# A table that moves 1119 operations in the instruction lists of a scheduled attention and two-MLP kernel

## The chip, the cores and the metric

The kernel runs on one core of one Trainium2 chip. The metric is the device time of one execution in microseconds (us). Five instruction lists run side by side, each strictly in its own order: TensorE (PE, matmuls), VectorE (DVE), ScalarE (ACT), GpSimd (POOL) and SyncE (SP, which issues every DMA here). An instruction at the head of a list that still waits for data holds up all that stand behind it.

## The reference

Three stages follow each other; all arrays are float32.

```python
# attention, 8 x 8 heads, 576 rows in chunks of 64, head size 64
scores = scale * np.matmul(q_c, k_c.transpose(0, 1, 2, 4, 3))
scores = scores - np.max(scores, axis=-1, keepdims=True)
attn = np.exp(scores)
attn = attn / (np.sum(attn, axis=-1, keepdims=True) + 1e-09)
out = np.matmul(attn, v_c)
# first MLP on 4608 tokens of 512: 512 -> 1536 (twice) -> 512
g = x @ w_gate
silu = g * (1.0 / (1.0 + np.exp(-g)))
x = silu * (x @ w_val) @ w_out
# second MLP: 512 -> 2048 -> 512
h = x @ w_in
g = h * (1.0 / (1.0 + np.exp(-1.702 * h)))
return g @ w_out
```

## The kernel before, in words

Tokens are worked in nine blocks of 512. There are four passes over all blocks: passes 0 and 1 hold six 128-wide slices each of `w_gate` and `w_val` and are the first MLP, passes 2 and 3 hold eight slices of `w_in` and are the second. Pass 0 also carries the attention: while PE multiplies block b, the 36 attention units of 128 tokens that feed the later blocks pass through it in small pieces (scores L662, values L667, transposes L732, the softmax on DVE at L715 to L723 with its exponential on ACT at L718). The first product of pass 0 starts at 23.0 us; the second MLP starts at 947.3 us and its second pass at 1303.9 us.

A float32 operand is split into a rounded high half and a remainder ("hi" and "lo"), and three matmuls take the place of one (`mm3`, L406 to L408). The high half is a copy on ACT (L390); the low half is a subtraction (`tt`, L399), on DVE or on POOL as the call says. Weights come from DRAM as 64-bit words and are made float32 on the core by two ACT and two DVE instructions (`conv_part`, L476 to L484). From the second block on, each 2x2 block product is done with seven multiplications in place of eight, so sums and differences of the weight quarters (`combos_from_quarters`) and of the token quarters (`token_combos`) have to be made first. The weights that later passes need are made during pass 0 and pass 2 and stored to DRAM (`group_to_dram`).

The order of all 6704 operations is set by a planner in the kernel, `Program`. Each operation is recorded with an engine, an estimated duration, a priority, and the operations it depends on. `order` lists the operations by priority and readiness under those estimates; `dues` works out latest times backwards, and the priorities are drawn towards them. This is repeated 28 times, each result is played through once more in `replay`, and the best of the 28 is emitted. The engine of an operation is fixed by the call that records it.

Of the kernel before, what the change touches and what calls it, by code (L numbers as in the profile page):

```python
# [24 lines left out]
def rd(ap):  # L25
    return ap.bitcast(F32)

# [68 lines left out]
class Program:  # L96
# [9 lines left out]
    ROUNDS = 14  # L106
    BEAT = 3.413
# [111 lines left out]
    def replay(self, seq, seed):  # L219
        jitter = random.Random(seed)  # L220
        queue = {eng: [] for eng in self.FREE}
        for o in reversed(seq):
            queue[o.eng].append(o)
            o.end = None
        free, table, port, owner, moved = dict(self.FREE), None, 0.0, None, 0.0
        busy, clock, beat = {}, 0.5, 0
        left, last = len(seq), 0.0
        while left:
            pick = None
            for eng, todo in queue.items():  # L230
                if not todo or any(d.end is None for d in todo[-1].deps):
                    continue
                o = todo[-1]
                s = max([free[eng], *(d.end + self.hop(d, o) for d in o.deps)])
                if pick is None or s < pick[0]:
                    pick = s, o
            s, o = pick
            queue[o.eng].pop()
            left -= 1
            us = o.us  # L240
            if o.eng == "dma":
                free["dma"] = s + 0.47
                moved = max(s + 1.5, moved) + 0.95 * us
                o.end = moved + 1.4 + max(-1.2, jitter.gauss(0, 0.8))
                continue
            if o.eng == "pe":
                while beat < s // self.BEAT:
                    share = busy.get(beat, 0.0) / self.BEAT
                    clock = 1.0 if share > 0.85 else 0.5 if share < 0.5 else clock
                    beat += 1  # L250
                if clock < 1.0 and us < 3.0:
                    us *= 1.8
                t = s
                while t < s + us:
                    k = t // self.BEAT
                    e = min(s + us, (k + 1) * self.BEAT)
                    busy[k] = busy.get(k, 0.0) + e - t
                    t = e + 1e-9
            if o.table and o.table != table:
                s, table = s + self.LOAD, o.table  # L260
            if o.port:
                us += abs(jitter.gauss(0, 0.02))
                o.end = max(s + 0.1, port + (self.HAND if o.eng != owner and port > s + 0.05 else 0.0)) + us - 0.1
                port, owner = o.end - 0.1, o.eng
            else:
                o.end = s + us
            free[o.eng] = o.end - (0.05 if o.eng != "pe" else 0.0)
            last = max(last, o.end)
        return last

    def emit(self):
        for o in self.ops:
            o.key, o.after = o.prio, []
        for o in self.ops:
            for d in (*o.deps, *o.follows):
                d.after.append(o)
        best = None
        for i in range(2 * self.ROUNDS):
            if i == self.ROUNDS:
                for o in self.ops:  # L280
                    o.key = o.prio
            seq = self.order()
            self.dues(seq)
            last = sum(self.replay(seq, j) for j in range(3)) / 3
            if best is None or last < best[0]:
                best = last, seq
            for o in self.ops:
                if o.prio < 9999:
                    o.key += (o.due - o.key) / (2 if i < self.ROUNDS else 4)
        for o in best[1]:  # L290
            o.fn()
# [3 lines left out]
def attention_two_moe_kernel(ctx: ExitStack, tc: tile.TileContext, q, k, v, wg, wv, wo, wi, wo2, out):  # L295
# [100 lines left out]
    def tt(dst, a, b, by, n, prio, eng="dve", of_a=lambda ap: ap, of_b=lambda ap: ap, near=None):  # L396
        e = nc.vector if eng == "dve" else nc.gpsimd
        op(eng, dve_us(n) if eng == "dve" else pool_us(n),
           lambda: e.tensor_tensor(out=dst.ap, in0=of_a(a.ap), in1=of_b(b.ap), op=by), [a, b], [dst], prio, near=near)  # L399
# [43 lines left out]
    for p, (layer, gs) in enumerate(passes):  # L443
        start.append([])
        for b in range(NB):
            start[p].append(t)
            t += sum(step_us(g) for g in gs) + (8.0 if p == 0 and b < NB - 1 else 0) + (3 * GV if p == b == 0 else 0)
# [244 lines left out]
    def scores(un, prio, done=None):  # L692
# [3 lines left out]
        if done is None:  # L696
            op("pe", 0.8, lambda: score_blocks(un), [un.q, un.k], [un.s], prio)
        else:
            done.o = right(t)

            def both_blocks():
                value_blocks(done)
                score_blocks(un)

            op("pe", 1.3, both_blocks, [done.v, done.e, un.q, un.k], [done.o, un.s], prio, near=1.0)
            attended(done, prio)
# [49 lines left out]
    def alone(un, prio):  # L756
        un.o = right(two(un))
        op("pe", 0.8, lambda: value_blocks(un), [un.v, un.e], [un.o], prio, near=1.0)
# [585 lines left out]
```

## Time and profile before

| what | value |
|---|---|
| median of 3 runs | 1688.71 us (1688.47 to 1689.58) |
| profiled execution | 1689.54 us, span 1687.2 us |
| PE busy | 1658.1 us (98% of the span) |
| PE weight loads busy | 1579.5 us (94%) |
| DVE busy | 1098.8 us (65%), 1606 instructions |
| ACT busy | 892.2 us (53%), 1511 instructions |
| POOL busy | 726.0 us (43%), 736 instructions |
| mean granted PE clock | 0.996 of full speed |

The profiled execution lies 0.83 us above the median; 2.3 us of it lie outside the span. PE is the bound nearly everywhere, so what matters is where it is not busy, or busy without being at its peak. Because matmuls overlap, a stalled PE can still be shown as busy; the weight-load column (PEld) is a second measure of it. PE's work is the same in both kernels.

### The profile page before, as it was taken

How to read it: one execution, taken by the hardware profiler on the slowest of the kernel's cores; microseconds unless marked ns; L12 is line 12 of the kernel's file. 1: busy time of each engine (PE TensorE's matmuls, PEld its weight loads, DVE VectorE, ACT ScalarE, POOL GpSimd, SP SyncE). 2: the span in 40 equal slices, each digit the busy share in tenths (PEclk: the TensorE clock that was granted, in tenths of full speed). 3: DMA queues.
4: the chain of work that ended last, by engine and by line, in shares of the span. 5: the costliest groups of instructions: out<-in, count | busy, mean ns of one | idle time of the engine just before them, and what ended most of it. 6: DMA issues, size and time to landing. Idle time of an engine off the chain costs nothing.

```text
span 1687.2 us, 36353 instructions
## 1 busy us (share of the span) xinstructions
PE 1658.1 (98%) x14428; PEld 1579.5 (94%) x14428; DVE 1098.8 (65%) x1606; ACT 892.2 (53%) x1511; POOL 726.0 (43%) x736
## 2 busy tenths in 40 slices
PE   7989999999999999999999999999999999999998
PEld 7878999889999999999999999999999999999998
DVE  6878877787764566644544477787755556555556
ACT  6876677777644444433333456555544444444443
POOL 2675516564444555541211235676731133333333
PEclk8999999999999999999999999999999999999999
DMA  7567788887899899887679998999989977777773
GB/s 293 177 237 276 271 273 301 284 288 258 281 333 342 305 330 325 304 283 243 233 247 337 375 334 299 312 318 317 311 262 339 348 231 232 233 238 236 235 257 109
DMA packets 184153, 472.65 MB, mean 280 GB/s; under 512 B 19760, under 2 KB 44848, under 8 KB 183728
## 3 DMA queue, kind: packets, MB, share of 16 engines
q1 hardware_dynamic: 183984, 470.34, 81.7%
q8 instruction: 114, 1.87, 0.4%
q14 instruction: 55, 0.45, 0.1%
HBM read 331.84 MB, written 138.41 MB: 279 GB/s over the span
## 4 chain that ended last, share of the span: by engine, by line
PE 84%; DVE 4%; DMA 3%; ACT 3%; issue 2%; POOL 2%; SPq 0%; POOLq 0%; DVEq 0%; ACTq 0%
PE banks L406 28%; PE banks L408 27%; PE banks L407 27%; PE banks L667 1%; DMA od_b<-ws 1%; DVE c L399 1%; PE banks L662 1%; DMA raw<-in_moe_w_out 1%; DVE xt L399 1%; DVE t L481 1%; PE banks L732 1%; ACT L718 0%; POOL ws L399 0%; DMA raw<-in_moe_w_in 0%; POOL wc L399 0%
## 5 line engine op out<-in xcount | busy, mean ns | idle before, releaser
L399 DVE TENSOR_TENSOR c<-u,banks 128x512 f32<-128x512 f32 x312 | 213.2, 683 | 307.4 <-PE banks L408 192.2
L406 PE MATMUL banks<-x,wc 128*128 128x256 f32 x1044 | 297.5, 285 | 3.2 <-ACT u L390 2.9
L407 PE MATMUL banks<-x,wc 128*128 128x256 f32 x1044 | 294.6, 282 | 0.0
L408 PE MATMUL banks<-x,wc 128*128 128x256 f32 x1044 | 294.5, 282 | 0.0
L390 ACT COPY u<-banks 128x512 f32<-128x512 f32 x261 | 152.9, 586 | 248.4 <-PE banks L408 247.2
L406 PE MATMUL banks<-x,wb 128*128 128x256 f32 x744 | 213.3, 287 | 4.2 <-ACT x L390 2.4
L406 PE MATMUL banks<-x,wa 128*128 128x256 f32 x744 | 211.3, 284 | 2.1 <-DVE c L399 1.6
L407 PE MATMUL banks<-x,wb 128*128 128x256 f32 x744 | 211.5, 284 | 0.8 <-DVE x L399 0.8
L408 PE MATMUL banks<-x,wb 128*128 128x256 f32 x744 | 211.4, 284 | 0.0
L407 PE MATMUL banks<-x,wa 128*128 128x256 f32 x744 | 210.0, 282 | 1.1 <-POOL x L399 1.1
L406 PEld LDWEIGHTS banks<-x,wc 128*128 128x128 f32 x1044 | 198.3, 190 | 13.2 <-ACT u L390 6.0
L408 PE MATMUL banks<-x,wa 128*128 128x256 f32 x744 | 210.0, 282 | 0.0
L407 PEld LDWEIGHTS banks<-x,wc 128*128 128x128 f32 x1044 | 198.4, 190 | 6.5
L408 PEld LDWEIGHTS banks<-x,wc 128*128 128x128 f32 x1044 | 198.9, 191 | 0.0
L406 PE MATMUL banks<-hh,o 128*128 128x512 f32 x432 | 173.5, 402 | 0.3 <-ACT hh L390 0.3
L408 PE MATMUL banks<-hh,o 128*128 128x512 f32 x432 | 172.6, 400 | 0.0
L407 PE MATMUL banks<-hl,o 128*128 128x512 f32 x432 | 170.8, 395 | 0.2 <-DVE hl L399 0.2
L974 ACT ACTIVATE xr<-c 128x512 f32<-128x512 f32 x136 | 86.0, 632 | 153.9 <-DVE c L399 149.8
L406 PEld LDWEIGHTS banks<-x,wb 128*128 128x128 f32 x744 | 142.7, 192 | 11.2 <-ACT x L390 2.5
L407 PEld LDWEIGHTS banks<-x,wb 128*128 128x128 f32 x744 | 142.8, 192 | 5.3 <-DVE x L399 1.0
L406 PEld LDWEIGHTS banks<-x,wa 128*128 128x128 f32 x744 | 141.0, 190 | 6.8 <-DVE c L399 2.8
L407 PEld LDWEIGHTS banks<-x,wa 128*128 128x128 f32 x744 | 140.9, 189 | 4.7 <-POOL x L399 1.7
(227 smaller groups left out, 4494.6 us busy)
## 6 DMA issues: line engine op xcount, KB each, us to landing
x<-x_dram SPq DMA_DIRECT2D x182, 512.0 KB, 5.5
o<-od_b SPq DMA_DIRECT2D x119, 512.0 KB, 4.6
o<-od_a SPq DMA_DIRECT2D x102, 512.0 KB, 5.1
x_dram<-x SPq DMA_DIRECT2D x56, 512.0 KB, 5.8
wd_b<-ws SPq DMA_DIRECT2D x56, 256.0 KB, 4.7
od_b<-ws SPq DMA_DIRECT2D x56, 256.0 KB, 4.6
raw<-in_moe_w_out SPq DMA_DIRECT2D x44, 255.8 KB, 4.8
wd_a<-ws SPq DMA_DIRECT2D x42, 256.0 KB, 4.2
```

Of the source, the lines that this page charges most:

```text
L390: op("act", act_us(n), lambda: nc.scalar.copy(out=dst.ap, in_=cut(src.ap)), [src], [dst], prio, near=near)
L399: lambda: e.tensor_tensor(out=dst.ap, in0=of_a(a.ap), in1=of_b(b.ap), op=by), [a, b], [dst], prio, near=near)
L406: nc.tensor.matmul(o, ah, bh, start=first, stop=False, **kind)
L407: nc.tensor.matmul(o, ah, bl, start=False, stop=False, **kind)
L408: nc.tensor.matmul(o, al, bh, start=False, stop=last, **kind)
L481: op("dve", dve_us(n), lambda: nc.vector.scalar_tensor_tensor(out=t.ap.bitcast(I32), in0=t.ap, scalar=-4096 * up, in1=word(1).bitcast(F32) ...
L662: nc.tensor.matmul(un.s.ap[h64(b), a, h64(g)], un.q.ap[h64(a), cs], un.k.ap[h64(a), cs], start=True, stop=True)
L667: nc.tensor.matmul(un.o.ap[h64(b), a, h64(2 * g + c)], un.v.ap[h64(a), cs], un.e.ap[h64(a), cs], start=True, stop=True)
L732: nc.tensor.transpose(pt.ap[:, cs], e.ap[:, cs], ident.ap)
L974: op("act", act_us(512), lambda: nc.scalar.activation(out=h.ap, in_=c.ap, func=AF.Gelu_apprx_sigmoid), [c], [h], prio, "gelu")
```

## The change

The 28 rounds, the replay and the choice among them are gone. Four rounds of `order` and `dues` make one list, and a table `PLACES` then changes it: for each engine, entries "behind : operations" take operations out of the list in which they stand and put them behind the named one. An entry may put an operation on another engine; only elementwise operations of `tt` go over, between DVE and POOL, and `tt` now looks up its engine when it emits. `amended` then merges the five lists again so that every operation comes after what it depends on. Three small estimates change too: the time set aside per block of pass 0 for attention (8.0 to 6.0) and the durations of the attention's PE pieces.

```diff
+PLACES = {
+    "pe": (
+        "6:44 8:25,28 61:27,21,5,7 22:26,23,10,9,78 52:16,69 24:17,13 71:12,15,14,11,20 86:18,95 244:103,210,105 "
...
-    ROUNDS = 14
-    BEAT = 3.413
+    ROUNDS = 4
+    BLEND = 2
...
-    def replay(self, seq, seed):
...
+    def amended(self, seq):
+        queue = {eng: [o for o in seq if o.eng == eng] for eng in self.FREE}
+        runs = [(eng, *run.split(":")) for eng, places in PLACES.items() for run in places.split()]
+        for eng, _, ns in runs:
+            for n in ns.split(","):
+                o = self.ops[int(n)]
+                queue[o.eng].remove(o)
+                o.eng = eng
+        for eng, behind, ns in runs:
+            i = queue[eng].index(self.ops[int(behind)]) + 1 if int(behind) >= 0 else 0
+            queue[eng][i:i] = [self.ops[int(n)] for n in ns.split(",")]
...
+        seq = self.order()
+        for i in range(self.ROUNDS):
             self.dues(seq)
...
+                    o.key += (o.due - o.key) / self.BLEND
+            seq = self.order()
+        for o in self.amended(seq):
             o.fn()
...
-        e = nc.vector if eng == "dve" else nc.gpsimd
-        op(eng, dve_us(n) if eng == "dve" else pool_us(n),
-           lambda: e.tensor_tensor(out=dst.ap, in0=of_a(a.ap), in1=of_b(b.ap), op=by), [a, b], [dst], prio, near=near)
+        o = op(eng, dve_us(n) if eng == "dve" else pool_us(n),
+               lambda: {"dve": nc.vector, "pool": nc.gpsimd}[o.eng].tensor_tensor(
+                   out=dst.ap, in0=of_a(a.ap), in1=of_b(b.ap), op=by), [a, b], [dst], prio, near=near)
...
-            t += sum(step_us(g) for g in gs) + (8.0 if p == 0 and b < NB - 1 else 0) + (3 * GV if p == b == 0 else 0)
+            t += sum(step_us(g) for g in gs) + (6.0 if p == 0 and b < NB - 1 else 0) + (3 * GV if p == b == 0 else 0)
```

In the two instruction lists, 169 operations that stood on POOL now stand on DVE and 38 went the other way, so DVE has 1737 operations where it had 1606, and POOL 600 where it had 731. Of the 169, 40 stood between 42 and 168 us of the trace of before (3 went the other way there) and 82 behind 1260 us. All five lists are reordered; line numbers of the changed kernel are 71 or 72 higher (L399 is L470, L390 is L462, L718 is L790).

The first place is the start, on DVE: the softmax of the third attention unit, whose last instruction (`c<-c,z`, L723 or L795) PE's next transposes need. Before:

```order
L481 SCALAR_TENSOR_TENSOR wc_200<-wc_200,wa_121 128x512 x2
L484 SCALAR_TENSOR_TENSOR wc_200<-wa_121,wc_200 128x512 x2
L719 TENSOR_REDUCE z<-c 128x8
L720 TENSOR_SCALAR z<-z 128x8
L722 RECIPROCAL z<-z 128x8
L723 TENSOR_TENSOR c<-c,z 128x512
L399 TENSOR_TENSOR x<-banks,x 128x4x128 x2
```

In the changed kernel, the same stretch of DVE's list:

```order
L556 SCALAR_TENSOR_TENSOR wc_217<-wa_117,wc_217 128x512
L553 SCALAR_TENSOR_TENSOR wc_217<-wc_217,wa_117 128x512
L556 SCALAR_TENSOR_TENSOR wc_217<-wa_117,wc_217 128x512
L791 TENSOR_REDUCE z<-c 128x8
L470 TENSOR_TENSOR x<-banks,x 128x4x128
L792 TENSOR_SCALAR z<-z 128x8
L794 RECIPROCAL z<-z 128x8
L470 TENSOR_TENSOR x<-banks,x 128x4x128
L795 TENSOR_TENSOR c<-c,z 128x512
```

The two token splits `x<-banks,x`, which stood behind that multiplication, now stand ahead of it.

The second place is a little later on ACT, around the copies `x<-banks` of the third and fourth unit. Before:

```order
L916 ACT_TABLE_LOAD
L916 ACTIVATE h<-banks 128x256
L478 ACTIVATE wb_273<-wb_273,offset 128x512 x2
L735 COPY c<-banks 128x512
L718 ACT_TABLE_LOAD
L718 ACTIVATE e<-e 128x512
L476 ACTIVATE t<-wa_318,offset 128x512
L390 CAST x<-banks 128x4x128
```

In the changed kernel:

```order
L462 COPY xr<-banks 128x4x128
L550 ACTIVATE wb_185<-wb_185,offset 128x512
L462 CAST x<-banks 128x4x128
L807 COPY c<-banks 128x512
L790 ACTIVATE e<-e 128x512
L988 ACT_TABLE_LOAD
L988 ACTIVATE h<-banks 128x256
L462 CAST x<-banks 128x4x128
```

The exponential `e<-e` has moved ahead of the first SiLU `h<-banks`, so that one table load is left between the copies where there were two.

The third place is POOL while the weights of the second block are made (`wc_1015` and the like are sums of weight quarters, `wa`, `wb`, `o` are low halves of weights). Before:

```order
L399 TENSOR_TENSOR wa_919<-wc_839,wa_919 128x2x256 x2
L399 TENSOR_TENSOR o<-t,o 128x512 x3
L399 TENSOR_TENSOR wc_1015<-raw,wc_1015 128x2x256
L399 TENSOR_TENSOR wc_1034<-ws,wc_1034 128x2x256
L399 TENSOR_TENSOR wc_1045<-raw,wc_1045 128x2x256
L399 TENSOR_TENSOR wb_293<-ws,wb_293 128x2x256
L399 TENSOR_TENSOR raw<-wc_358 128x512
L399 TENSOR_TENSOR raw<-raw,wc_544 128x512
L399 TENSOR_TENSOR ws<-wc_544,wc_358 128x512
```

In the changed kernel, POOL's list from its second weight to the first token quarters of the second block:

```order
L470 TENSOR_TENSOR wa_361<-wc_284,wa_361 128x2x256
L470 TENSOR_TENSOR wa_608<-wc_414,wa_608 128x2x256
L470 TENSOR_TENSOR wc_825<-raw,wc_825 128x2x256
L470 TENSOR_TENSOR wc_829<-raw,wc_829 128x2x256
L470 TENSOR_TENSOR o<-t,o 128x512 x2
L470 TENSOR_TENSOR wc_1083<-raw,wc_1083 128x2x256
L470 TENSOR_TENSOR x<-xr,x 128x512
```

Ahead of its first `x<-xr,x` POOL has ten subtractions and sums where it had 34; the others, such as the sums `raw` and most low halves, stand on DVE now.

## Rows read from the trace of the kernel before

**Rows 1.** Busy time by stretch, the whole core
```profile
core 0: us, PE busy (x) PEld busy (x) DVE busy (x) ACT busy (x) POOL busy (x), PEclk, DMA share, GB/s
0.00:42.00 42.00, 32.01 (x438) 29.52 (x439) 29.00 (x50) 29.26 (x47) 8.38 (x14) 0.88 0.77 294
42.00:84.00 42.00, 39.85 (x442) 35.81 (x441) 34.11 (x49) 37.49 (x61) 26.60 (x20) 1.00 0.54 174
84.00:126.00 42.00, 37.53 (x446) 32.71 (x445) 33.15 (x46) 29.62 (x47) 31.95 (x23) 1.00 0.70 242
126.00:168.00 42.00, 40.05 (x499) 36.20 (x498) 34.96 (x53) 28.76 (x49) 25.02 (x26) 1.00 0.78 273
252.00:294.00 42.00, 42.00 (x460) 38.52 (x459) 32.11 (x53) 30.09 (x49) 24.98 (x28) 1.00 0.86 297
168.00:1638.00 1470.00, 1466.98 (x12270) 1404.29 (x12269) 939.53 (x1373) 750.04 (x1282) 617.29 (x645) 1.00 0.85 289
```

**Rows 2.** What PE waited for, 0 to 42 us (total, times, longest)
```profile
PE banks L732 <- DVE c L723: 4.0, 2, 3.6
PE banks L406 <- ACT x L390: 2.4, 1, 2.4
PE banks L407 <- DVE x L399: 0.8, 1, 0.8
```

**Rows 3.** ACT in order of time, 29 to 37 us (start, duration)
```profile
30.13 1.28 ACT L916 ACT_TABLE_LOAD   x1
33.60 1.28 ACT L718 ACT_TABLE_LOAD   x1
36.07 0.57 ACT L390 CAST x<-banks 128x512 fp32r<-128x512 f32 x1
```

**Rows 4.** POOL in order of time, 78 to 101 us
```profile
78.52 2.85 POOL L399 TENSOR_TENSOR o<-t,o 128x512 fp32r<-128x512 f32 x2 [3.06 <-ACT o L390]
96.85 1.74 POOL L399 TENSOR_TENSOR wb<-ws,wb 128x512 fp32r<-128x512 f32 x1
98.56 2.97 POOL L399 TENSOR_TENSOR x<-xr,x 128x512 fp32r<-128x512 f32 x2
```

**Rows 5.** What PE waited for, 42 to 168 us
```profile
PE banks L406 <- ACT u L390: 2.9, 3, 1.4
PE banks L732 <- DVE e L723: 1.4, 1, 1.4
PE banks L407 <- POOL x L399: 1.1, 1, 1.1
```

**Rows 6.** POOL's groups by shape, 42 to 168 us (busy us, mean ns)
```profile
L399 POOL TENSOR_TENSOR x<-xt,x 128x512 fp32r<-128x512 f32 x6 | 9.7, 1620 | 0.0
L399 POOL TENSOR_TENSOR wc<-raw,wc 128x512 fp32r<-128x512 f32 x6 | 7.7, 1295 | 9.9 <-ACT wc L390 9.9
```

**Rows 7.** DVE's groups by shape, 42 to 168 us
```profile
L723 DVE TENSOR_TENSOR e<-e,z 128x512 f32<-128x512 f32 x10 | 12.3, 1229 | 0.3
L399 DVE TENSOR_TENSOR hl<-h,hh 128x512 fp32r<-128x512 f32 x12 | 10.6, 892 | 1.4 <-ACT hh L390 1.4
L399 DVE TENSOR_TENSOR c<-u,banks 128x512 f32<-128x512 f32 x13 | 8.8, 678 | 0.1
```

**Rows 8.** One DVE multiplication of that shape, 11 us, POOL idle
```profile
11.16 0.69 DVE L723 TENSOR_TENSOR e<-e,z 128x512 f32<-128x512 f32 x1
```

**Rows 9.** What PE waited for, 168 to 1680 us
```profile
PE banks L406 <- DVE c L399: 1.6, 3, 1.0
```

**Rows 10.** The end, all engines in order of time
```profile
1679.73 0.28 PE L408 MATMUL banks<-wb,xt 128*128 128x256 f32 x1
...
1681.02 2.48 POOL L399 TENSOR_TENSOR t<-t,e 128x512 f32<-128x512 f32 x2
...
1682.31 0.69 DVE L399 TENSOR_TENSOR t<-t,banks 128x512 f32<-128x512 f32 x1
1683.03 0.91 SPq L386 DMA_DIRECT2D out<-t  x2
```

More of the change, by code (lines that the diff above doesn't have):

```diff
@@ L1 @@
 import heapq
-import random
 from contextlib import ExitStack
@@ L26, in rd @@
     return ap.bitcast(F32)
+PLACES = {
[18 rows of a table added]
+    ),
+    "dve": (
[31 rows of a table added]
+    ),
+    "act": (
[16 rows of a table added]
+    ),
+    "pool": (
[7 rows of a table added]
+    ),
+    "dma": (
[21 rows of a table added]
+    ),
+}
 class Buf:
@@ L217, in dues @@
                     heapq.heappush(heap, (-d.end, -d.n, d))
-    def replay(self, seq, seed):
[L220 to L237, printed above, removed]
-            queue[o.eng].pop()
[L239 to L269, printed above, removed]
@@ new lines, in amended @@
+    def amended(self, seq):
[9 more added lines that the diff above has]
+            queue[eng][i:i] = [self.ops[int(n)] for n in ns.split(",")]
+        rank = {o: i for i, o in enumerate(seq)}
+        for todo in queue.values():
+            last = len(seq)
+            for o in reversed(todo):
+                last = rank[o] = min(rank[o], last)
+            todo.reverse()
+        made = set()
+        while len(made) < len(seq):
+            heads = [todo[-1] for todo in queue.values() if todo and made.issuperset(todo[-1].deps) and made.issuperset(todo[-1].follows)]
+            o = min(heads, key=lambda o: (rank[o], o.n))
+            queue[o.eng].pop()
+            made.add(o)
+            yield o
@@ L276, in emit @@
                 d.after.append(o)
[L277 to L282, printed above, removed]
+        seq = self.order()
+        for i in range(self.ROUNDS):
             self.dues(seq)
-            last = sum(self.replay(seq, j) for j in range(3)) / 3
-            if best is None or last < best[0]:
-                best = last, seq
             for o in self.ops:
                 if o.prio < 9999:
-                    o.key += (o.due - o.key) / (2 if i < self.ROUNDS else 4)
-        for o in best[1]:
+                    o.key += (o.due - o.key) / self.BLEND
+            seq = self.order()
+        for o in self.amended(seq):
             o.fn()
@@ L696, in scores @@
         if done is None:
-            op("pe", 0.8, lambda: score_blocks(un), [un.q, un.k], [un.s], prio)
+            op("pe", .72, lambda: score_blocks(un), [un.q, un.k], [un.s], prio)
         else:
@@ L703, in both_blocks @@
                 score_blocks(un)
-            op("pe", 1.3, both_blocks, [done.v, done.e, un.q, un.k], [done.o, un.s], prio, near=1.0)
+            op("pe", 1.18, both_blocks, [done.v, done.e, un.q, un.k], [done.o, un.s], prio, near=1.0)
             attended(done, prio)
@@ L757, in alone @@
         un.o = right(two(un))
-        op("pe", 0.8, lambda: value_blocks(un), [un.v, un.e], [un.o], prio, near=1.0)
+        op("pe", .72, lambda: value_blocks(un), [un.v, un.e], [un.o], prio, near=1.0)
         attended(un, prio)
```

91 rows, old and new, of the table PLACES are left out of this document.

## The prediction

> **What bounds the kernel now.** I read the busy time by stretch first. From 168 to 1638 us PE is busy 1466.98 of 1470 us [rows 1]: PE's own work is the bound there, it is the same in both kernels, and nothing that is moved between the other engines can take more than about 3 us from these 1470. The idle time lies at the two ends. From 0 to 42 us PE is idle 10.0 us and the granted clock is 0.88; from 42 to 168 us it is idle 2.15, 4.47 and 1.95 us; and behind its last matmul at 1680.0 us the span goes on for 7.2 us [rows 1, 10].
>
> Between 42 and 168 us the idle time understates the loss, since a stalled PE can still count as busy. The weight loads show it: in a stretch of the same pass where PE is never idle they are busy 38.52 of 42 us, but here 35.81, 32.71 and 36.20 [rows 1]. That is 104.72 against 115.56, short by 10.84, which at 38.52 per 42 us is 11.8 us of PE time lost in these 126.
>
> Then I read who makes PE wait. At the start it is the softmax of the third attention unit (one wait of 3.6 us) and later a copy of token parts on ACT (2.4 us) [rows 2]; between the two stand two table loads of ACT, 1.28 us each, before the copy at 36.07 us [rows 3]. From 42 to 168 us the waits themselves are short and scattered: 2.9 us on ACT's copies of partial sums, 1.4 on a softmax, 1.1 on a token quarter from POOL [rows 5]. Behind them POOL works almost without a gap from 78.5 us on: it ends the second block's weights at 98.6 us and only then begins its tokens [rows 4]. DVE runs 33 to 35 of 42 us, but part of that is waiting too. A multiplication of two SBUF tiles takes 0.69 us while POOL is idle [rows 8] and 1.229 us on average here, the low half `hl` 0.892, while an addition that reads PSUM stays at 0.678 [rows 7]. So DVE and POOL stretch each other's work when both read SBUF alone, and POOL's own subtraction runs from 1.295 to 1.620 us for one shape [rows 6].
>
> **The change part by part.** Times are summed against the profiled execution, 1689.54 us (span 1687.2 plus 2.3 outside); it stands 0.83 us above the median of 1688.71.
>
> *Start, 0 to 42 us.* In PE's new list the third unit's transposes still stand ahead of the first product. On DVE 23 instructions stand ahead of the multiplication that they need, where there were 21, for the two token splits went in front. At 0.69 us each that is 1.4 us later; beside POOL at 1.229 it is 2.5 [rows 7, 8]. Against that, one of the two table loads before the next token copy is gone: 1.28 us off a wait of 2.4 [rows 2, 3]. I book 0. The ends are a loss of 2.5 and a gain of both later waits, 2.4 + 0.8 = 3.2 us.
>
> *42 to 168 us.* Of POOL's operations 40 go to DVE and 3 come back. At the mean of its two rows, 1.46 us, POOL loses 58 us and gains 4, so its 83.6 busy us in the three stretches become about 30 [rows 1, 6]: the row of weights that ends at 98.6 us is no longer a row. DVE takes 37 more at 0.69, or 25.5 us, on top of 102.2 busy us: 127.7 in 126 us, if nothing else changed. But its stretching shrinks with POOL's share. The two stretched groups alone lose 10 x 0.54 and 12 x 0.20, together 7.8 us in 22 of DVE's 148 instructions [rows 1, 7, 8]; with POOL at 30 of 83.6 some 5 us of that go, and if the other operations on two SBUF tiles are stretched alike, an estimate of three times as much, 15. That leaves DVE between 113 and 123 us of work for a stretch that would be 114 us long with no loss at all. DVE is therefore what is late next, and the whole 11.8 us is unlikely to come back. But it is idle 23.8 of the 126 us now [rows 1], which covers the 25.5 us less the 5 to 15 that shrink. I take three quarters: 8.8 us. The ends are 0 and 11.8.
>
> *168 to 1680 us.* PE is idle 3.0 us up to 1638 [rows 1], the largest item 1.6 us in three waits on DVE's sums [rows 9]. 82 of the moves from POOL to DVE lie behind 1260 us, where PE hides everything; they cost nothing as long as DVE, busy 939.53 of 1470 us, is not asked for two late results at once. I take 1 us gained. The ends are a loss of 4 (each of the three long passes finds one new wait of about the longest here, 1.0 us, and one more) and a gain of 3.
>
> *The end.* Now two last additions on POOL take 2.48 us, to 1683.5, the last DVE addition runs to 1683.0, and the two DMAs issued from 1683.0 close the span [rows 10]. In the new lists one DVE addition of 0.69 us stands behind the last matmul, and POOL's last addition needs a sum that is ready one product earlier. The last stores can be issued about 1 us sooner. I take 1 us; the ends are 0 and 1.5.
>
> Sum: 0 + 8.8 + 1 + 1 = 10.8. The profiled time becomes 1678.7, the median 1677.9; I say 1678 us. All good ends together give 3.2 + 11.8 + 3 + 1.5 = 19.5 us, or 1669.2.
>
> **The rivals.**
>
> *The loss only changes its owner.* ACT is busy 37.49 of 42 us from 42 to 84 us, more than any engine but PE [rows 1], and the longest waits in the stretch are on its copies [rows 5]. If ACT's list is what holds PE, then POOL's relief gives back little. Against it: from 84 us on ACT has 12 us of slack per stretch, while the loss is largest there (37.53 busy). I give it 3 us in the middle and half of the end: 1688.7 - 3 - 0.5 = 1685.
> The Trainium skill has a rule that speaks for this one (Perfetto Trace Analysis, section Optimizing Scalar/DVE Operations): GpSimd and VectorE share an SBUF read port, so that handing operations between those two "might not help". By that rule the middle term is 0 and the time 1687.
> The trace bears out the shared port [rows 7, 8], but not the price: an operation holds it 1.295 us or more on POOL and 0.69 on DVE, so the exchange frees about half of it.
>
> *DVE becomes the bound (slower).* Place: 42 to 168 us. If DVE's instructions stay as stretched as they are, since the few left on POOL meet them all the same, it has 127.7 us to do. It has never been busier than 34.96 of 42 us (0.83) in these rows; at a generous 0.92 the stretch takes 138.8 us, 12.8 more than now, and with 2 us from the other terms the time is 1699.5. It decides from the point where DVE's busy share in the three stretches passes 0.92. Against it: softmax and gating on DVE read PSUM or an ACT result for half of their instructions, which are not stretched at all [rows 7].
>
> *New waits in the saturated passes.* All five lists are reordered over the whole kernel, and PE has no reserve from 168 us on: each wait is paid in full. Nine blocks in each of the last two passes with half a microsecond apiece cost 9 us and cancel the gain: 1688.7 - 10.8 + 9 = 1687. For it: lists are shuffled far from any wait. Against it: PE's waits there came to 3 us in 1470, so the slack of the chains around it is large.
>
> **How the numbers follow.** The forecast of a gain near 10.8 us has 0.67, with its own range 1671 to 1683. The change of owner has 0.18 at 1685, the new waits 0.07 at 1687, DVE as the bound 0.08 at 1699.5. What this measurement can tell from no change is 0.2%, 3.4 us, so faster means below 1685.3 and slower above 1692.1. Faster: 0.67, half of the second (0.09) and a little of the third (0.03), 0.79. Slower: 0.08 and a little, 0.09. The rest, 0.12, is no difference. The range of 8 in 10 takes the forecast with its good end and the change of owner: 1669 to 1687.
>
> **What would show it.** Right: PEld busy in the 42 us stretches up to 168 near 38, POOL near a third of its time there, DVE near 37 of 42 with L723's mean down towards 0.8 us; the second block's products well before 98 us; the last matmul near 1670 and less than 6.5 us behind it. Wrong: PE waits on DVE (`hl`, `x`, softmax) of several us between 50 and 130 us with DVE above 0.92 would make it the bound; waits spread over the later passes, with PE busy below 1464 in the 1470 us, would mean new waits; no shorter start together with ACT above 37 of 42 would mean that ACT was the limit.

## The result and the profile after

The changed kernel takes 1673.12 us (median of 4 runs, 1670.53 to 1674.76) where the kernel before took 1688.59 in the same series: ratio 0.9906, 95% interval 0.9889 to 0.9924. That is 15.5 us less, where the forecast was 10.8 less. The profiled execution is the quickest of the four, 1670.53 us with a span of 1668.7, so differences read between the two traces add up to some 18.5 us and not to 15.5.

The busy time by stretch of the changed kernel, to be held against [rows 1]:

```profile
core 0: us, PE busy (x) PEld busy (x) DVE busy (x) ACT busy (x) POOL busy (x), PEclk, DMA share, GB/s
0.00:42.00 42.00, 34.33 (x538) 31.77 (x539) 32.94 (x61) 32.54 (x56) 7.73 (x13) 0.96 0.82 310
42.00:84.00 42.00, 41.10 (x433) 36.18 (x435) 40.33 (x73) 38.73 (x65) 7.47 (x6) 1.00 0.50 167
84.00:126.00 42.00, 42.00 (x572) 38.40 (x565) 38.14 (x66) 29.70 (x51) 11.85 (x10) 1.00 0.82 283
126.00:168.00 42.00, 39.86 (x437) 35.89 (x436) 32.64 (x58) 27.62 (x46) 11.85 (x16) 1.00 0.90 318
...
168.00:1638.00 1470.00, 1468.26 (x12276) 1407.46 (x12275) 960.64 (x1454) 737.72 (x1273) 507.67 (x557) 1.00 0.83 287
```

POOL's busy time in the three stretches from 42 to 168 us has fallen from 83.6 to 31.2 us, DVE's has risen from 102.2 to 111.1. The weight loads (PEld) rise by 0.4, 5.7 and minus 0.3 us there: nearly all of the middle's gain is in the stretch in which before made the second block's weights and tokens.

What PE waited for in the changed kernel (total, times, longest), first 0 to 42 us, then 42 to 168, then 168 to 1680; these answer to [rows 2, 5, 9]:

```profile
PE banks L804 <- DVE c L795: 1.8, 1, 1.8
PE banks L739 <- ACT wc L548: 1.8, 1, 1.8
...
PE banks L478 <- DVE c L470: 1.7, 1, 1.7
PE banks L479 <- DVE hl L470: 0.8, 1, 0.8
...
PE banks L478 <- DVE c L470: 1.1, 3, 0.6
```

The longest wait is half of the 3.6 us before, and the 2.4 us on ACT's token copy are gone. But the listed waits explain only part of the gain. A better ruler is PE's own steps, which are the same in both kernels: when does each begin? A step is found in every kernel by counting the matmuls of 256 columns.

| step of PE | before, us | after, us | earlier by |
|---|---|---|---|
| first product of pass 0 | 23.00 | 21.25 | 1.75 |
| its ninth product | 46.87 | 41.21 | 5.66 |
| first seven-multiplication product (second block) | 98.47 | 88.62 | 9.85 |
| the 29th of these | 173.12 | 160.52 | 12.60 |
| first of the second MLP | 947.28 | 930.86 | 16.42 |
| start of the last matmul | 1679.73 | 1661.12 | 18.61 |
| end of the span | 1687.2 | 1668.7 | 18.5 |

So the start gives about 5.7 us, the middle 6.9, everything behind it 6.0, and the end nothing. The forecast had 0, 8.8, 1 and 1.

This is one trace of each kernel, and the start differs from trace to trace. In the three kernels that begin with the old list and engines (before, and below the one with the addresses alone and the one with only the later part) the ninth product starts at 46.87, 45.72 and 44.60 us. In six that begin with the new ones (the changed kernel and its repeat, only the start, up to the 29th, late back, last stores) it starts between 40.00 and 41.21 us. So the start's gain is between 3.4 and 6.9 us.

### The profile page after: what moved, and what is told of

It is laid out like the page before. It is cut to its first block, busy times and chain, and to the rows that moved or that the text cites. A ratio compares the mean times of both kernels' runs of the same rounds, so it can differ in the third digit from the quotient of the medians.

```text
span 1668.7 us, 36144 instructions
## 1 busy us (share of the span) xinstructions
PE 1648.9 (99%) x14428; PEld 1572.6 (94%) x14428; DVE 1123.5 (67%) x1737; ACT 875.7 (52%) x1503; POOL 552.0 (33%) x605
## 4 chain that ended last, share of the span: by engine, by line
PE 91%; DVE 4%; ACT 1%; DMA 1%; issue 1%; POOL 0%; SPq 0%; DVEq 0%; POOLq 0%; ACTq 0%
PE banks L478 30%; PE banks L480 29%; PE banks L479 29%; PE banks L739 1%; PE banks L734 1%; PE banks L804 1%; DVE c L470 0%; DMA hh<-in_q 0%; DMA x_dram<-q 0%; DMA wd_b<-ws 0%; DVE t L553 0%; DVE m L787 0%; DVE z L791 0%; DVE hl L470 0%; DVE h L470 0%
## 5 line engine op out<-in xcount | busy, mean ns | idle before, releaser
L470 DVE TENSOR_TENSOR c<-u,banks 128x512 f32<-128x512 f32 x312 | 213.1, 683 | 257.7 <-PE banks L480 149.0
L462 ACT COPY u<-banks 128x512 f32<-128x512 f32 x261 | 152.8, 585 | 270.0 <-PE banks L480 269.1
L478 PE MATMUL banks<-x,wb 128*128 128x256 f32 x744 | 211.0, 284 | 0.8 <-ACT u L462 0.4
L479 PE MATMUL banks<-x,wb 128*128 128x256 f32 x744 | 209.4, 282 | 0.0
L480 PE MATMUL banks<-x,wb 128*128 128x256 f32 x744 | 209.3, 281 | 0.0
L478 PEld LDWEIGHTS banks<-x,wb 128*128 128x128 f32 x744 | 141.0, 190 | 7.1 <-ACT u L462 1.5
L479 PEld LDWEIGHTS banks<-x,wb 128*128 128x128 f32 x744 | 141.0, 189 | 4.0
```

The costliest lines, as they stand in the source:

```text
L462: op("act", act_us(n), lambda: nc.scalar.copy(out=dst.ap, in_=cut(src.ap)), [src], [dst], prio, near=near)
L470: lambda: {"dve": nc.vector, "pool": nc.gpsimd}[o.eng].tensor_tensor(out=dst.ap, in0=of_a(a.ap), in1=of_b(b.ap), op=by), [a, b], [dst], pr ...
L478: nc.tensor.matmul(o, ah, bh, start=first, stop=False, **kind)
L479: nc.tensor.matmul(o, ah, bl, start=False, stop=False, **kind)
L480: nc.tensor.matmul(o, al, bh, start=False, stop=last, **kind)
```

## The experiments

Each compares with the kernel before on the same chip in the same series (medians there 1689.2 to 1689.7 us); all do the same computation. First the changed kernel once more.

> The changed kernel itself, as the mark for the others. Its four runs so far lie between 1670.5 and 1674.8 us, so 1672 to 1674 us and a ratio to before of 0.989 to 0.992 are expected by every theory. Its spread (over 4 us) is wider than that of before (1.7 us): if it comes from when the first loads land, the runs differ in the first 20 us alone.

Measured: 1672.95 us (1670.35 to 1676.62), ratio 0.9901 [0.9886, 0.9916]. The gain repeats.

**The four rounds without the table.** The lists of `order` are emitted as they are.

```diff
-        for o in self.amended(seq):
+        for o in seq:
```

> The changed kernel without its table: four rounds of ordering, nothing moved, no operation on another engine. Theory: the gain is the table's, and a list made by estimates alone is no better than the best of 28, so 1686 to 1700 us. Rival: the four rounds with the smaller estimates (6.0 us per block, shorter attention pieces) already make most of the gain: at most 1678 us.

Measured: 1690.4 us, ratio 1.0007 [0.9998, 1.0016]. The smaller estimates and the fewer rounds give nothing; the table gives all of it.

**All 207 operations back on their engines.** The table's places in the lists are kept.

```diff
+        o.hold, o.home = self.hold, eng
...
-        for o in self.amended(seq):
+        for o in list(self.amended(seq)):
+            o.eng = o.home
```

> The changed kernel with its order, but all 207 operations that changed between DVE and POOL back on their old engine, each at the same place in the merged order. Theory: relieving POOL is what matters between 42 and 168 us; POOL is busy over 70 us there again, and 6 to 9 us come back: 1679 to 1683 us. Rival (the order of the lists matters, the engine doesn't): 1672 to 1675 us. Second rival: POOL's 1.3 to 1.6 us in chains laid out for 0.7 also hurts in the last passes: above 1690 us.

Measured: 1691.31 us, 1.0012 [1.0003, 1.0021]: 18.4 us come back and not 6 to 9, the time of the second rival. The first product of the second block starts at 100.30 us, 11.7 us later than in the changed kernel, and from the second MLP's first step to the last matmul it takes 738.9 us where the changed kernel takes 730.3. The new order is worth nothing without the new engines. The reverse, the new engines in the old order, was not run, so what the moves are worth without the new places is not shown.

**Only the 43 of 42 to 168 us back.**

```diff
+        back = set(map(int, BACK.split()))
...
+            if o.n in back:
+                o.eng = o.home
```

> The changed kernel with only the 43 operations back on their old engine that stood between 42 and 168 us in the trace of before (40 to POOL, 3 to DVE). Theory: these are the ones that matter, 1678 to 1682 us, within 1.5 us of the kernel with all of them back. Rival (the order matters): 1672 to 1675 us. If the run with all back is slow and this one is not, the moves outside that stretch count.

Measured: 1683.4 us, 0.9961 [0.9948, 0.9973], 10.4 us above the changed kernel. What PE waits for from 42 to 168 us in this kernel, and behind it two waits of ACT and DVE from 58 to 92 us:

```profile
PE banks L488 <- DVE hl L479: 4.0, 2, 3.7
PE banks L813 <- DVE e L804: 2.6, 1, 2.6
...
DVE wc L562 <- ACT wc L559: 2.4, 1, 2.4
ACT wc L471 <- POOL ws L479: 2.1, 1, 2.1
```

PE waits for DVE although DVE's list holds 37 operations fewer, and ACT and DVE wait in their turn: ACT stands behind a difference of weights that POOL makes late, DVE behind ACT. POOL is busy 29.0 us from 42 to 84 us again, 7.5 in the changed kernel, and the clock is no longer full there (the figure behind POOL's is the granted clock, 1.00 in both other kernels):

```profile
42.00:84.00 42.00, 36.56 (x353) 31.81 (x346) 35.49 (x45) 32.03 (x54) 29.02 (x20) 0.92 0.46 157
```

The first product of the second block starts at 99.36 us, 10.7 us later than in the changed kernel, so the whole loss lies ahead of it. A part of it is the clock: 0.92 over 42 us is 3.4 us of full speed, an estimate, and the fall stands behind PE's 3.7 us wait. So in the new order relieving POOL is what moves the middle; that ACT, from which nothing is moved, is late only behind POOL is read from the waits. The 10.4 us are the worth of the moves in an order that needs them: the kernel before, with POOL just as busy, has its own order and a full clock there.

**Only the start.** The kernel before, with the changed kernel's order and engines (5 swaps) for all that stands ahead of the ninth product, 199 operations.

```diff
-        for o in best[1]:
+        early = [self.ops[int(n)] for n in EARLY.split()]
+        for n in SWAP.split():
+            self.ops[int(n)].eng = {"dve": "pool", "pool": "dve"}[self.ops[int(n)].eng]
+        done = set(early)
+        for o in early + [o for o in best[1] if o not in done]:
```

> The kernel before, with the changed order (and its 5 changes of engine) for everything that stands ahead of the ninth weight product on PE, and its own order from there on. That product started at 46.87 us before and at 41.21 us in the changed kernel. Theory: time won at the start stays won, because PE is the bound behind it: 1683 to 1685 us. Rival: the stretch from 42 to 168 us is bound by POOL's row of weights, which is not relieved here, so the early start is given back there: 1687 to 1690 us.

Measured: 1681.07 us, 0.9955 [0.9941, 0.9968]: 8.6 us, more than expected. In this trace the ninth product starts at 40.33 us, 6.5 us earlier than before, the 29th of the second block's at 166.03, 7.1 us earlier, and the last matmul 8.5 us earlier. So nothing is given back in the middle, and more is won behind it; why comes with the last experiment.

**The same up to the 29th seven-multiplication product** (747 operations, 46 swaps; the code is the same).

> The kernel before, with the changed order and engines for everything ahead of the 29th seven-product step of PE (started at 173.12 us before, at 160.52 in the changed kernel), its own order behind. Theory: 12.4 us of the gain lie ahead of that point and stay: 1676 to 1678 us, and the 4 us up to the changed kernel are the later order's. Rival: nothing behind 173 us matters, as the forecast had it: within 1 us of the changed kernel, 1672 to 1674 us.

Measured: 1676.42 us, 0.9919 [0.9906, 0.9933]. From the 29th product on this is the old list. The changed kernel's median is 3.5 us lower, but the two intervals overlap. By the starts of the steps the difference lies in the first MLP: from the 29th product to the second MLP it takes 774.5 us here and 770.3 in the changed kernel (771.8 in its repeat), from there to the last matmul 731.0 against 730.3 (731.1). What PE waits for from 168 to 1650 us in this kernel:

```profile
PE banks L449 <- ACT u L433: 2.1, 2, 1.2
PE banks L449 <- DVE c L441: 1.6, 3, 1.1
```

With 0.7 us in two smaller ones that is 4.4 us, against 1.5 us in the changed kernel: the old list, begun 12 us earlier, runs into waits that the new one avoids.

**Only the later part.** The changed kernel, with the old order and the old engines up to the same step (751 operations).

```diff
+        rest = list(self.amended(seq))
+        early = [self.ops[int(n)] for n in EARLY.split()]
+        for o in early:
+            o.eng = o.home
+        done = set(early)
+        for o in early + [o for o in rest if o not in done]:
```

> The reverse of the run with the changed order up to 173 us: here the old order and old engines stand ahead of the 29th seven-product step, and the changed order and engines behind. Theory: it keeps what the later order is worth, 1673.0 against 1676.4, or 3 to 4 us: 1685.5 to 1687 us. Rival: the later order only fits the earlier start and brings nothing by itself: 1689 to 1691 us.

Measured: 1692.04 us, 1.0017 [1.0008, 1.0026]: not a gain but a small loss. ACT and DVE in this kernel, where the two lists meet (start, duration, operation, idle time and what ended it):

```profile
172.82 0.52 ACT L586 ACTIVATE t<-raw,offset 128x256 f32<-128x256 int16 x1 [2.11 <-DMA raw<-in_moe_w_val]
...
173.98 0.43 DVE L591 SCALAR_TENSOR_TENSOR t<-t,raw 128x256 int32<-128x256 f32 x1 [3.94 <-ACT raw L588]
```

The new list has a weight conversion at the head of both engines there whose data, in the old timing, come late; DVE's sums queue behind it and PE waits 3.1 us for one of them (5.2 us in three such waits from 168 to 1650 us). The later order is not better in itself. It fits the earlier start.

**The 107 moves behind 1260 us undone**, by the same lines as for the middle.

> The changed kernel with the 107 operations back on their old engine that stood behind 1260 us in the trace of before (82 to POOL, 25 to DVE), order as it is. The prediction booked these moves at nothing. With all 207 back the time was 1691.3 us, with the 43 of the middle alone 1683.4, so 8 us belong to the other 164. Theory: the new order leaves short waits behind 1000 us when POOL takes 1.3 us for a step where 0.7 was laid out, so 4 to 7 us of the 8: 1677 to 1680 us, with PE idle spread over the last two passes. Rival (the prediction): PE hides them, 1672 to 1674 us.

Measured: 1677.99 us, 0.9937 [0.9924, 0.9949], 5.0 us above the changed kernel. The last stretch of this kernel:

```profile
1260.00:1638.00 378.00, 376.05 (x3133) 373.23 (x3132) 222.25 (x304) 167.47 (x287) 116.05 (x87) 1.00 0.73 253
```

and of the changed one:

```profile
1260.00:1638.00 378.00, 378.00 (x3165) 376.62 (x3164) 245.81 (x364) 169.87 (x291) 46.70 (x34) 1.00 0.74 254
```

PE does 32 matmuls fewer in the same 378 us, 3.8 us of work at 0.119 us each; the waits listed there, on ACT's and DVE's sums, come to 1.7 us, the rest is in pieces too short for the list. The kernel before, which has none of the moves but its own order, did 3152 there. From the second MLP's first step to the last matmul it takes 736.6 us here, 730.3 in the changed kernel and 732.5 in the kernel before.

**The clock at the start.** The kernel before, with 16 matmuls of `ident`, whose results nobody reads, where PE idles ahead of the third unit's transposes.

```diff
+    def fill():
+        for i in range(16):
+            nc.tensor.matmul(units0[3].both.ap[:, 0, 256:384], ident.ap, ident.ap, start=True, stop=True)
```

> The kernel before with 16 idle matmuls of the identity added on PE behind the second unit's values, where PE idled 3.8 us from 17.4 us on and the granted clock then was at half speed from 21.2 to 28.1 us; order and engines unchanged. Theory: with PE kept going the clock stays at full speed and the first product takes 1.4 us where it took 2.7; 1 to 2.5 us are won in all: 1686.5 to 1688.5 us. Rival: the later wait on ACT's token copy at 36 us swallows it: no change within 0.5 us.

Measured: 1687.39 us, 0.999 [0.9981, 0.9999], 2.3 us less (0.2 to 3.2). In the kernel before, the granted clock (the figure behind POOL's) is halved, to 1.2 GHz, for most of the 7 us that follow PE's 3.6 us wait:

```profile
21.00:28.00 7.00, 6.11 (x27) 5.71 (x28) 6.04 (x11) 4.98 (x9) 2.15 (x2) 0.52 1.01 405
28.00:38.00 10.00, 6.11 (x129) 5.38 (x127) 7.81 (x16) 8.89 (x13) 0.37 (x1) 1.00 0.36 122
38.00:42.00 4.00, 4.00 (x21) 4.00 (x22) 2.51 (x4) 3.99 (x8) 2.59 (x2) 0.57 0.61 252
```

with the added matmuls:

```profile
21.00:28.00 7.00, 5.84 (x102) 5.40 (x101) 6.05 (x10) 6.18 (x12) 2.31 (x2) 1.00 1.02 407
28.00:38.00 10.00, 6.56 (x66) 5.62 (x66) 8.45 (x17) 9.93 (x15) 1.16 (x2) 0.82 0.61 222
38.00:42.00 4.00, 4.00 (x23) 4.00 (x22) 3.75 (x5) 4.00 (x8) 2.17 (x3) 0.58 0.02 6
```

and in the changed kernel, where the wait itself is shorter:

```profile
21.00:28.00 7.00, 4.79 (x108) 4.42 (x99) 6.69 (x12) 6.52 (x13) 2.99 (x2) 0.89 1.03 415
28.00:38.00 10.00, 10.00 (x104) 9.71 (x104) 8.73 (x18) 8.73 (x15) 0.00 (x0) 0.90 0.61 241
38.00:42.00 4.00, 3.98 (x85) 3.51 (x84) 3.83 (x7) 4.00 (x9) 1.05 (x1) 1.00 0.52 162
```

The added matmuls remove the first fall, and a later one is longer. Their ninth product starts at 45.0 us, 1.9 us earlier than before, but this profiled execution is the slowest of its 11 (1689.95 us), so the gain in time rests on the medians alone. In the changed kernel a shorter wait at the start is paid back twice: PE begins earlier, and at the full 2.4 GHz for most of the time.

**The last five stores in another order.** The changed kernel, with two stores of `yv` ahead of those of `t` whose sums come last.

```diff
+        made = list(self.amended(seq))
+        d = [o for o in made if o.eng == "dma"][-5:]
+        made = [o for o in made if o not in d] + [d[i] for i in (2, 4, 3, 0, 1)]
```

> The changed kernel with its last five stores issued in another order: the three whose data are ready first go ahead of the two that wait for the last additions. Theory: the predicted gain of 1 us at the end did not come because five stores queued behind the latest one; from the last matmul to the end of the span 7.3 us become 5.2 to 6.0, and the time goes to 1671 to 1672 us. Rival: the last landing is set by the last addition alone: 7 us stay.

Measured: 1670.63 us (1668.86 to 1671.99), 0.9889 [0.9876, 0.9903], the quickest kernel here, 2.3 us below the changed one; the two intervals overlap, but the traces show where it lies. The end of the changed kernel (start, duration, operation; it answers to [rows 10]):

```profile
1661.12 0.28 PE L480 MATMUL banks<-wb,xt 128*128 128x256 f32 x1
1661.50 0.69 DVE L470 TENSOR_TENSOR t<-t,banks 128x512 f32<-128x512 f32 x1 [0.20 <-issue]
1662.08 1.45 SPq L458 DMA_DIRECT2D out<-t  x3
1663.62 1.19 SPq L458 DMA_DIRECT2D out<-yv  x2
```

and with the stores reordered:

```profile
1660.62 1.68 SPq L461 DMA_DIRECT2D out<-yv  x2
...
1661.73 0.28 PE L483 MATMUL banks<-wb,xt 128*128 128x256 f32 x1
1662.10 0.69 DVE L473 TENSOR_TENSOR t<-t,banks 128x512 f32<-128x512 f32 x1 [0.20 <-issue]
1662.69 0.92 SPq L461 DMA_DIRECT2D out<-t  x2
```

In the changed kernel five stores stand in a row in SP's list behind the last sum, and each takes SP about half a microsecond to issue; two of them (`yv`) could have gone earlier. From the start of the last matmul the span goes on for 7.6 us there and for 5.3 us here (it ends at 1667.0).

**That, and fillers in the changed kernel's own gap.** Eight `ident` matmuls (two records each) behind the fifth unit's scores, where PE idles 1.8 us.

```diff
+        for i in range(8):
+            nc.tensor.matmul(units0[3].both.ap[:, 0, 256:384], ident.ap, ident.ap, start=True, stop=True)
```

> The changed kernel with the last five stores in the better order and with 8 idle matmuls of the identity on PE behind the fifth unit's scores, where PE idled 1.8 us from 24.5 us on and the granted clock then was at half speed from 26.5 to 29.9 us. Theory: the clock stays at full speed there and about 1 to 1.5 us are won beside the 2.3 of the stores: 1669 to 1670 us. Rival: the fourth unit's softmax on DVE holds the following steps anyway, so nothing beside the stores: 1670.5 to 1671 us.

Measured: 1675.89 us, 0.9929 [0.9917, 0.9942], 5.3 us worse than without the fillers, which neither the theory nor the rival had. PE and DVE in it:

```profile
24.49 2.05 PE L1376 MATMUL banks<-ident 128*128 128x128 f32 x16
26.58 0.69 DVE L793 TENSOR_TENSOR c<-banks,m 128x512 f32<-128x512 f32 x1 [3.77 <-PE banks L1376]
...
29.96 0.63 PE L809 MATMUL banks<-ident,c 128*128 128x128 f32 x4 [3.42 <-DVE c L800]
```

The fillers write a part of the bank from which DVE still has to take the fourth unit's softmax, so DVE waits 3.77 us for them and PE in turn 3.42 us for DVE. Whether fillers in a bank of their own would help the changed kernel was not tried.

**The buffers' addresses alone.** The traces held one more difference. The mean distance from the start of a matmul of 256 columns to the next start, from 500 to 900 us, distances over 200 ns left out, worked out from some 2150 records each:

| order of the first 40 us | kernels | ns |
|---|---|---|
| not the table's | before, no table, 16 fillers, later part only | 119.03, 119.03, 119.04, 119.07 |
| the table's | changed, start only, to the 29th, engines back, middle back, late back | 118.85, 118.79, 118.78, 118.82, 118.86, 118.82 |

PE waits for next to nothing there, and what it does is the same. But a ring of buffers gets its SBUF address when its first buffer is used, so the order of the first 40 us sets where all weights and tokens lie for the whole program. The last run is the kernel before, operation for operation, with the rings laid out as in the changed one.

```diff
+        for tag in self.places.split():
+            self.ring[tag].made[0].ap
         for o in best[1]:
             o.fn()
...
+        prog.ring, prog.places = ring, (
+            "k q hh hl wa1 m wb1 v e c wb2 z wc1 wc0 wc2 wa2 wc5 wc6 wb0 x xr wc4 wa0 wc7 wc8 wc3 ws h t raw o xt yv u st")
```

> The kernel before, with every operation on its engine and in its place in all five lists. Only the SBUF addresses of the ring buffers change: a ring gets its address when its first buffer is used, and here the rings are asked for their first buffer, ahead of the first instruction, in the sequence in which the changed kernel comes to them (so the weight ring wb1 lies behind m instead of behind wc1, and so on). Theory, from the traces so far: two matmuls of 256 columns that follow each other without a wait start 119.0 to 119.1 ns apart (500 to 900 us) in every kernel that starts with the old list (before, the four rounds without the table, the fillers, the later order alone) and 118.8 to 118.9 in every one that starts with the new list, also where all behind the start is the old list; so the pace hangs on where the weights lie. By this theory the mean distance falls to 118.8 to 118.9 here, which over 14428 matmuls is 2.2 to 3.2 us: 1686 to 1687.5 us against 1689.3. Rival: the pace comes from how the engines stand to each other after an earlier start; then the distance stays at 119.05 and the time within 1 us of before, 1688.5 to 1690.

Measured: 1687.11 us (1684.82 to 1690.19), 0.9983 [0.9972, 0.9993]; the distance is 118.79 ns. Two of the three matmuls with `wb`, 500 to 900 us, in the kernel before (busy us, mean ns):

```profile
L408 PE MATMUL banks<-x,wb 128*128 128x256 f32 x208 | 58.6, 282 | 0.0
L407 PE MATMUL banks<-x,wb 128*128 128x256 f32 x208 | 58.6, 282 | 0.0
```

and the same two in the kernel with only the addresses changed:

```profile
L409 PE MATMUL banks<-x,wb 128*128 128x256 f32 x208 | 58.4, 281 | 0.0
L410 PE MATMUL banks<-x,wb 128*128 128x256 f32 x208 | 58.3, 280 | 0.0
```

In the changed kernel their means are 281 and 280 ns too. By the starts of all three, the distances behind a matmul with `wb` were 118.06, 119.16 and 119.05 ns before; they are 118.74, 118.02 and 117.69 with the addresses changed, and 118.91, 118.05 and 117.83 in the changed kernel. Those with `wc` agree within 0.15 ns in all three kernels. Of the 14428 matmuls, all of which the expectation counted, 10620 have 256 columns; 0.24 ns on each is 2.5 us. The run shows 2.1, with an interval of 1.2 to 4.7. The kernel with only the start has the new pace too (118.79 ns), so addresses are part of its 8.6 us.

## Why the prediction was right, and where it was not

The direction held, the time fell into the range, and the mechanism of the middle term, POOL's relief, is there. But only that term is near its size. Two booked at 0 and 1 came out near 6 each, beyond their own good ends of 3.2 and 3, and the one at the end came out at 0. That the time still lies in the range is in part luck: the range added up all the good ends, and the middle's 11.8, of which little more than half came, left room for what the other two brought beyond theirs.

*Start: booked 0, measured about 5.7 us by the ninth product (3.4 to 6.9 over the traces); the term failed, and its bound of 3.2 too.* The step was: 23 instructions stand ahead of the third unit's multiplication where there were 21, so it comes 1.4 to 2.5 us later. The count is right. But it says nothing of when DVE begins and how long each instruction takes. DVE before:

```profile
17.87 0.68 DVE L719 TENSOR_REDUCE z<-c 128x8 f32<-128x512 f32 x1
18.58 0.80 DVE L720 TENSOR_SCALAR z<-z 128x8 f32<-128x8 f32 x1
...
19.66 1.48 DVE L723 TENSOR_TENSOR c<-c,z 128x512 f32<-128x512 f32 x1
```

and after:

```profile
16.11 0.68 DVE L791 TENSOR_REDUCE z<-c 128x8 f32<-128x512 f32 x1
...
17.30 0.16 DVE L792 TENSOR_SCALAR z<-z 128x8 f32<-128x8 f32 x1
...
18.76 0.68 DVE L795 TENSOR_TENSOR c<-c,z 128x512 f32<-128x512 f32 x1
```

The first scores come 1.2 us earlier on PE (5.57 us, before 6.77), behind one of the kernel's own idle matmuls of `ident` where four stood, and DVE's first instruction with them (6.52, before 7.88); and the multiplication takes 0.68 us where it took 1.48, the tiny one ahead of it 0.16 where it took 0.80. The two token splits cost their time, and the multiplication is still ready 1.7 us sooner. This part is not sure to be the table's: in the kernel with only the later part, which begins with the old list, the scores start at 5.67 us and the multiplication is ready at 19.35, as early as in the changed kernel (19.44). Only 1.75 of the 5.66 us lie ahead of the first product.

What stands in every trace is the rest. The table load was read rightly: one stands there now, and the token copy behind it starts at 30.56 instead of 36.07:

```profile
28.41 1.28 ACT L988 ACT_TABLE_LOAD   x1
...
30.56 0.59 ACT L462 CAST x<-banks 128x512 fp32r<-128x512 f32 x1 [0.33 <-PE banks L739]
```

The wait of 2.4 us on that copy, in all three traces that begin with the old list, is in none of the six with the new one. The prediction took 1.28 us off it and set that against a loss on DVE. What it left out altogether was the clock, although [rows 1] had the 0.88: the changed kernel has 0.96 there, and the run with added matmuls puts 2.3 us (0.2 to 3.2) on one fall of it.

*42 to 168 us: booked 8.8, measured 6.3 by the weight loads* (110.47 less 104.72, times 42 / 38.52), 6.9 by PE's steps. The mechanism held in its parts: POOL 31.2 us (said: about 30), DVE 111.1 (said: 113 to 123), the second block's products 9.85 us earlier. So did the stretching. DVE's rows by shape, 42 to 168 us, against [rows 7]:

```profile
L470 DVE TENSOR_TENSOR c<-u,banks 128x512 f32<-128x512 f32 x17 | 11.5, 678 | 0.6 <-PE banks L480 0.5
L470 DVE TENSOR_TENSOR hl<-h,hh 128x512 fp32r<-128x512 f32 x13 | 9.5, 729 | 0.9 <-ACT hh L462 0.8
L795 DVE TENSOR_TENSOR e<-e,z 128x512 f32<-128x512 f32 x11 | 9.1, 824 | 0.2
```

The two that read SBUF alone went from 1229 to 824 and from 892 to 729 ns, the one that reads PSUM stayed at 678. The term is too large by a third because half of the loss came back and not three quarters. From 42 to 84 us DVE is busy 0.96 of the time: it is indeed late next. From 126 to 168 us nothing came back, and one of the three moves to POOL has a hand in it. DVE and POOL there:

```profile
127.81 1.29 POOL L470 TENSOR_TENSOR xt<-xr 128x512 f32<-128x512 f32 x1 [11.10 <-ACT xr L462]
...
129.14 0.69 DVE L470 TENSOR_TENSOR xt<-xr,xt 128x512 f32<-128x512 f32 x1 [2.15 <-POOL xt L470]
```

DVE idles 2.15 us for a difference that POOL makes in 1.29, and some microseconds later PE waits 1.7 us for a sum of DVE. That the one leads to the other was read from the trace and not tried.

*168 to 1680 us: booked 1, measured 6.0; mis-sized, and its bound of 3 as well.* Some 2.6 us are the distance between matmuls, which no step of the prediction had: from 168 to 1638 us it falls from 119.12 to 118.96 ns behind some 9700 matmuls of 256 columns, and from 234.7 to 233.8 behind some 1150 of 512. The rest is put down to the later order, worth 3.5 us (with overlapping intervals) between the kernel with the new order up to the 29th product and the changed one, and only together with the earlier start. That the 82 moves behind 1260 us cost nothing held. But in the new order they are not idle either, since undoing them, with the 25 the other way, costs 5.0 us. Against the kernel before they win little, for with its own order it lost little there (732.5 us from the second MLP's first step to the last matmul, against 730.3). The moves pay for an order that needs them.

*The end: booked 1, measured 0; the step failed.* It followed the last sum and not what SP has to do behind it. Reordering five stores gives 2.3 us.

*The rivals.* That the loss only changes its owner to ACT falls: ACT rose to 38.73 of 42 us from 42 to 84, yet PE waited for it only 0.5 us from 42 to 168, and putting 43 operations back, none of them ACT's, costs 10.4 us.
The Trainium skill's rule behind this rival (Perfetto Trace Analysis, section Optimizing Scalar/DVE Operations), that moving operations between GpSimd and VectorE "might not help", is not borne out: with the same, new order, the 207 moves are worth 18.4 us (1691.31 less 1672.95).
DVE as the bound came close in one stretch (0.96) and not over the three (0.88). New waits in the later passes did appear where the new order ran without its moves or without its start, and not in the kernel as a whole.

What the 16.7 us between 1689.66 and the repeated 1672.95 are made of, adding the table's parts in the order of the program: the start 8.6, of which about 2 are addresses; up to the 29th product another 4.7; all later 3.5, within the noise of four runs each. The steps of PE divide it as 5.7, 6.9 and 6.0, because there the addresses, which the runs charge to the start, count where they act.

## What to carry to other kernels

Order and engine go together: here neither the new order on the old engines, nor its later half alone, was worth anything (the new engines in the old order were not tried), so test a schedule's parts from the front and expect the rest to need the earlier start. For a move between VectorE and GpSimd, count what it takes off the slower engine and off the other's stretching, not the operations. When something changes the order in which buffers are first used, compare the distance between matmuls where nothing waits, and give the last stores of a queue the order in which their data come.

## What the hardware showed that was not expected

The SBUF addresses of the operands change TensorE's pace: 119.03 against 118.79 ns from start to start with the same instructions in the same order, 2.1 us of the program's time. Which property of an address does it (distance between the rings, their offset within some unit) stays open.

The four runs of the changed kernel in one series lie between 1670.35 and 1676.62 us. Its clock does not fall at the same place each time: in the first profiled execution it is below full from 21 to 38 us (0.89 and 0.90, shown above), in the repeat's from 14 to 21 us (0.76) and full from 21 to 35, and with the stores reordered, where PE's list up to there is the same, full throughout. This alone does not make the spread: the repeat's trace is 1.7 us longer than the first, but its ninth product starts earlier (40.57 us against 41.21) and its second MLP later (931.71 against 930.86). The cause stays open.
